# Three fp32 layers on one core: weight conversions beside attention through GpSimd's queue, low words rounded on GpSimd, and a table of leads that orders the ready work

## The chip, the core and the metric

The kernel runs on one core of a Trainium2 chip. Five engines take part, each with an instruction queue of its own: TensorE (PE in the profile; its weight loads are PEld), VectorE (DVE), ScalarE (ACT), GpSimd (POOL) and SyncE (SP), which here issues transfers only. The metric is the device time of one launch in microseconds, the lower the better.

## The reference

```python
scores = scale * np.matmul(q, k.transpose(0, 1, 3, 2)) - np.log(S)   # 4 x 12 heads, S = 448, head_dim 64
attn = 1.0 / (1.0 + np.exp(-scores))
attn_out = np.matmul(attn, v).astype(np.float32)
x = np.ascontiguousarray(attn_out.transpose(0, 2, 1, 3)).reshape(B * S, H * D)   # 1792 tokens x 768
h = x @ w_in                     # 768 x 2048
x = (h * np.cos(h)) @ w_out      # 2048 x 768
g = x @ w_gate                   # 768 x 1536
silu = g * (1.0 / (1.0 + np.exp(-g)))
val = x @ w_val
out = silu * val @ w_out2        # 1536 x 768
```

Sigmoid attention, then a layer with h cos(h), then a gated layer. q, k and v are float32; the five weights come as float64.

## The kernel before

**Precision.** A float32 operand is held as a pair of fp32r tiles, `hi` (a rounded copy) and `lo` (what the copy left out), and a product is three matmuls, hi hi, hi lo and lo hi. Making such a pair takes a copy (mostly on ScalarE) and a subtraction on VectorE.

**Weights.** They lie in memory as 64-bit words. A loop in `conversions` (L419) makes float32 of one tile of 128 x 768 after the other: load the raw words (768 KB, `raw` or `lr`), round the low word to float32 (L430, ScalarE), take the absolute value of the high word (`absolute`, L412, ScalarE or VectorE), clamp it (L435), shift it (L438), put sign and bits together (L441), add the low word as an integer (a custom instruction, `vec` at L230), and store the tile (384 KB) to scratch memory, where `loads` fetches it again whenever a unit wants it. Two such loops run through the MLP; beside attention `lend_pool` (L388) runs four more with tiles `lr0` to `lr3` and `lt0` to `lt3`, which convert 13 tiles. All their transfers are issued by SyncE (`move`, L235), in whose queue the loads of q and k (`rqk`) and v (`vs`) stand too.

**Attention.** 24 pairs of heads, one after the other. VectorE splits the next pair's q and k into `qk` (L723, L724; two buffers), TensorE makes four blocks of scores (L734), ScalarE the sigmoid `a` (L738), and TensorE weighs v with the pair before (L748, sums in `banks`). The pair's output is copied into `R` (rows `r`).

**MLP.** TensorE works through 28 units of two tiles of d_ff; units 0 to 7 are the first layer's first half of the tokens, 8 to 15 its second half, from 16 on comes the second layer. Half and layer together are a stage. A unit is seven products (numbers 1 5 2 6 7 3 4, nine matmuls each of 128 x 448) of sums of operand blocks, which stand for eight plain ones, and between them the down products of the unit before (twelve matmuls each), which need all four `g`. For each unit VectorE and ScalarE make the weight operands (`wa`, `wb`, `s` and one tile in `x1`), and of each result `g`: u, f, the rounding (L816), a sine, a product, the pair `g`. At a change of stage they also make the seven operands `X` of the next stage's tokens from `R` (`inputs`, L640 on): four subtractions into `R`, seven copies `hi` (L658 ScalarE, L660 VectorE) and seven subtractions `lo`, each over 3 x 448 columns. A slot of `X` comes free when its last product of the stage before is done; the last stage's unit still has its down products ahead.

**Order.** Everything beside attention is placed by a list scheduler at build time (`Order`, L74 on). Steps are generators that yield an engine (or several) with an estimated time; of the ready steps the one that can start first is taken, and among equals the one of lowest rank. A rank is mostly a due time in TensorE's plan less a lead that is written out in the code.

```python
key = (start, task.rank)
if best is None or key < best[0]:
    best = key, task, engine, time
```

The program order of each engine is thereby fixed; on the chip an engine that waits holds up all that stands behind it in its own queue. In attention the hand-written steps stand first and the scheduler fills the time between them (`beside`).

## Time and profile before

| what | value |
|---|---|
| median of 3 runs | 1082.96 us (1081.62 to 1082.97) |
| profiled execution | 1087.36 us, span of its core 1085.3 us |
| granted TensorE clock, mean | 0.992 of 2.4 GHz |
| busy: TensorE, VectorE, ScalarE, GpSimd | 98%, 78%, 61%, 11% |
| transfers of SyncE's queue | 155.51 MB, 45.3% of the 16 DMA engines' time |

Times in the rows are from the span's start. Attention takes the first 154 us, the first layer goes to 586 us, the second to the end. The profiled execution is some 4 us longer than the median. Busy shares are averages; where an engine holds up another is read from waits and timeline.

### The profile page before, as it was taken

What the parts mean: (1) busy time and instruction counts of PE and PEld (TensorE: products, weight loads), DVE (VectorE), ACT (ScalarE), POOL (GpSimd) and SP (SyncE); (2) the same over time, 40 slices, a digit from 0 to 9 for tenths busy, and PEclk for the clock granted to TensorE, in tenths of its full rate; (3) what the DMA queues carried; (4) which work ended last, traced back from release to release, by engine and by line L of the source; (5) the groups of instructions that cost most, each with busy time, mean ns of one, the idle gap of its engine ahead of it and who ended that gap; (6) DMA issues with size and microseconds to landing.
All of it is one profiled execution on the core that took longest, in us unless ns stands there. A gap on an engine that the chain in (4) does not pass through costs nothing.

```text
span 1085.3 us, 14759 instructions
## 1 busy us (share of the span) xinstructions
PE 1065.9 (98%) x5507; PEld 933.1 (86%) x5507; DVE 848.9 (78%) x1138; ACT 664.8 (61%) x1005; POOL 124.7 (11%) x97
## 2 busy tenths in 40 slices
PE   9999999999999899999997999999999999999998
PEld 5554569999989799999997999999999999999997
DVE  4969759989999999989899888897559644555643
ACT  6887768877777777777776665554345344433330
POOL 0000002001111101100023100111111210110100
PEclk9999999999999899999998999999999999999999
DMA  9999424545654145454513565655122322112002
GB/s 267 301 264 248 143 88 146 200 150 175 220 202 146 59 161 205 160 188 146 189 59 122 170 221 202 203 189 175 45 73 76 117 85 73 56 48 73 30 1 102
DMA packets 64455, 156.68 MB, mean 144 GB/s; under 512 B 10112, under 2 KB 36736, under 8 KB 64384
## 3 DMA queue, kind: packets, MB, share of 16 engines
q1 hardware_dynamic: 64240, 155.51, 45.3%
q8 instruction: 43, 0.70, 0.3%
q10 hardware_dynamic: 144, 0.23, 0.1%
q14 instruction: 28, 0.23, 0.1%
HBM read 123.47 MB, written 32.24 MB: 143 GB/s over the span
## 4 chain that ended last, share of the span: by engine, by line
PE 88%; DVE 9%; issue 1%; ACT 1%; DMA 0%; DVEq 0%; ACTq 0%
PE banks L1000 42%; PE banks L902 33%; PE banks L748 7%; PE banks L734 6%; DVE x L230 2%; DVE r L230 2%; DVE u L230 1%; DVE g L230 1%; DVE wa L230 1%; DVE wb L230 0%; DMA rqk<-in_qk 0%; DVE u L816 0%; DVE s L230 0%; DVE x L660 0%; ACT x L658 0%
## 5 line engine op out<-in xcount | busy, mean ns | idle before, releaser
L902 PE MATMUL banks<-g,wb 128*128 128x448 f32 x1044 | 224.2, 362 | 1.1 <-ACT g L227 0.6
L1000 PE MATMUL banks<-x,wb 128*128 128x448 f32 x1044 | 224.9, 363 | 0.3 <-ACT banks L227 0.3
L902 PEld LDWEIGHTS banks<-g,wb 128*128 128x128 f32 x1044 | 195.5, 187 | 15.5 <-ACT g L227 1.4
L1000 PEld LDWEIGHTS banks<-x,wb 128*128 128x128 f32 x1044 | 196.8, 189 | 14.0 <-ACT banks L227 0.7
L902 PE MATMUL banks<-g,wa 128*128 128x448 f32 x720 | 160.6, 370 | 9.8 <-ACT g L227 8.5
L1000 PE MATMUL banks<-x,wa 128*128 128x448 f32 x738 | 159.7, 362 | 0.1
L902 PEld LDWEIGHTS banks<-g,wa 128*128 128x128 f32 x720 | 137.9, 192 | 21.3 <-ACT g L227 9.3
L1000 PEld LDWEIGHTS banks<-x,wa 128*128 128x128 f32 x738 | 138.2, 187 | 10.3 <-issue 0.7
L227 ACT ACTIVATE u<-u 128x448 f32<-128x448 f32 x179 | 99.4, 570 | 39.4 <-DVE u L230 26.6
L230 DVE TENSOR_TENSOR u<-u,banks 128x448 f32<-128x448 f32 x119 | 73.4, 617 | 57.1 <-PE banks L1000 54.1
L230 DVE TENSOR_TENSOR r<-banks,r 128x896 f32<-128x896 f32 (+1 forms) x69 | 74.2, 1075 | 50.5 <-PE banks L902 50.0
L738 ACT ACTIVATE a<-banks 128x896 f32<-128x896 f32 x96 | 82.9, 920 | 20.2 <-PE banks L734 12.4
L230 DVE TENSOR_TENSOR wb<-t,wb 128x768 fp32r<-128x768 f32 x73 | 69.5, 956 | 14.9 <-ACT wb L227 14.4
L227 ACT ACTIVATE g<-u 128x448 fp32r<-128x448 f32 x97 | 55.1, 572 | 39.0 <-DVE u L230 23.9
L1000 PE MATMUL banks<-x,s 128*128 128x448 f32 x360 | 78.5, 362 | 0.0
L734 PEld LDWEIGHTS banks<-qk 64*128 64x128 f32 x576 | 51.5, 188 | 29.6 <-ACT a L738 8.2
L227 ACT ACTIVATE wb<-t 128x768 fp32r<-128x768 f32 x73 | 60.9, 837 | 24.6 <-PE banks L1000 17.8
L512 POOL TENSOR_TENSOR sum<-t 128x384 f32<-128x384 f32 x20 | 35.2, 1758 | 339.9 <-DMA t<-swi 78.1
L734 PE MATMUL banks<-qk 64*128 64x448 f32 x576 | 69.9, 386 | 3.5 <-ACT a L738 2.2
L227 ACT ACTIVATE r<-banks 128x896 f32<-128x896 f32 x52 | 47.8, 920 | 41.1 <-PE banks L902 41.0
L1000 PEld LDWEIGHTS banks<-x,s 128*128 128x128 f32 x360 | 67.5, 188 | 4.5
L227 ACT ACTIVATE banks<-banks 128x448 f32<-128x448 f32 x80 | 42.3, 529 | 46.3 <-PE banks L1000 45.1
(103 smaller groups left out, 1476.3 us busy)
## 6 DMA issues: line engine op xcount, KB each, us to landing
raw<-in_w_out SPq DMA_DIRECT2D x23, 768.0 KB, 5.2
t<-swi SPq DMA_DIRECT2D x32, 384.0 KB, 3.2
t<-swo SPq DMA_DIRECT2D x64, 192.0 KB, 2.5
rqk<-in_qk SPq DMA_DIRECT2D x47, 224.0 KB, 7.5
raw<-in_w_gate SPq DMA_DIRECT2D x12, 768.0 KB, 4.6
raw<-in_w_val SPq DMA_DIRECT2D x12, 768.0 KB, 4.9
t<-swg SPq DMA_DIRECT2D x18, 384.0 KB, 3.0
t<-swd SPq DMA_DIRECT2D x34, 192.0 KB, 3.0
```

Source lines behind the costliest of these rows:

```text
L227: return {"ACT": time}, lambda _: nc.scalar.activation(**kw)
L230: return {"DVE": time}, lambda _: nc.vector.tensor_tensor(out=out, in0=in0, in1=in1, op=op)
L512: on.tensor_tensor(out=out, in0=a, in1=b, op=op)
L734: nc.tensor.matmul(sc[:, j], lhsT=both[half, m, 1, starts[c]:starts[c] + P], rhs=both[half, p, 0], start=n == 0, stop=n == 2,)
L738: nc.scalar.activation(out=a, in_=sc, func=AF.Sigmoid, bias=-math.log(S), scale=1.0 / math.sqrt(D))
L748: nc.tensor.matmul(o[half], lhsT=value, rhs=a[:, j], start=c == 0, stop=c == NCH)
L902: nc.tensor.matmul(banks[:, first + e - d, :N], lhsT=w[:, m, e % KH, :], rhs=g[:, 1 - p], start=(i, m, p) == (0, 0, 0) and is_fresh and no ...
L1000: nc.tensor.matmul(bank, lhsT=w[:, m, k, :], rhs=x[p][:, k], start=(k, m, p) == (0, 0, 0) and i in (1, 5), stop=(k, m) == (KH - 1, 1), ski ...
```

## The change

In the three parts of the title, and with new estimates for some steps:

- **Queue.** The loops beside attention issue their raw loads and their stores on GpSimd (`move_beside`), and the plan gives a raw load 9.5 us to land. `begun` lets the four loops begin 4.5 us apart, each behind a one-element copy by GpSimd that reads a tile of q and k. 14 tiles are converted there (13 before), 54 in the MLP (55).
- **Rounding.** The low word is multiplied by 2^-29 and turned into float32 by a `tensor_scalar` of GpSimd in place of ScalarE's activation: 68 instructions.
- **Leads.** The leads come from a table, `LEAD`, whose entries take the place of the numbers in the code; the estimate of a cast of `x` on VectorE goes from 0.9 to 1.55 us, and a product's from 0.203 to 0.2005 a matmul.

TensorE's own order of products is the same. Counted by engine: VectorE casts five `x` (nine before), ScalarE copies 23 (19); VectorE takes 19 absolute values fewer and ScalarE as many more; GpSimd has 68 roundings, 28 transfers and 4 copies more; SyncE has 26 transfers fewer. The other leads are replaced in the same way as the ones shown.

```diff
+LEAD = {
+    "u": 4.53,
+    "f": 4.5,
+    "stt": 3.8,
+    "sin": -0.47,
+    "mult": 2.8,
+    "ghi": -0.12,
+    "glo": 1.06,
+    "whi": 12.36,
+    "wlo": 4.37,
+    "c5": -2.88,
+    "c7": 6.95,
+    "c6": 2.87,
+    "c3": 4.46,
+    "xd": 5.72,
+    "xhi": -8.03,
+    "xlo": -0.1,
+    "sv": 15.9,
+    "acc": -1.59,
+    "bank": 1.82,
+    "first": 1.35,
+    "second": 3.8,
+    "fifth": -3.28,
+    "s22": 6.97,
+    "s12": 6.23,
+    "silu": 3.11,
+    "conv": 21.66,
+}
...
+    def move_beside(out, in_):
+        return {"POOL": 0.9}, lambda _: nc.gpsimd.dma_start(out=out, in_=in_)
+
     LANDING = 5.0
+    LANDING_BESIDE = 9.5
...
-    PRODUCT = 0.203
+    PRODUCT = 0.2005
...
-                uses.setdefault((id(w), 2 * c + i), due[key] - 25.0)
+                uses.setdefault((id(w), 2 * c + i), due[key] - LEAD["conv"])
...
-    def lend_pool():
+    def lend_pool(raw_qk):
...
-            order.spawn(conversions(raw, t, backs[-1], stop), end)
+            order.spawn(begun(a, raw_qk, conversions(raw, t, backs[-1], stop)), end)
...
+    def begun(a, raw_qk, steps):
+
+        yield 6.0 + 4.5 * a
+        yield {"POOL": 0.3}, lambda _: nc.gpsimd.tensor_copy(warm[:, a:a + 1], raw_qk[:, (a + 1) % 4, 1, S - 1:S])
+        yield from steps
...
-        return {"ACT": 0.9, "DVE": 0.58}, do
+        return {"ACT": 0.9, "DVE": 0.61}, do
...
-            yield move(raw.rearrange("p n two -> p (n two)"), flat(w[f]).bitcast(I32))
-            yield LANDING
-            yield by(time, act(0.9, out=raw[:, :, 0], in_=raw[:, :, 0].bitcast(U32), func=AF.Copy, scale=2.0 ** -29))
+            convey = move_beside if back else move
+            yield convey(raw.rearrange("p n two -> p (n two)"), flat(w[f]).bitcast(I32))
+            yield LANDING_BESIDE if back else LANDING
+            yield by(time, ({"POOL": 1.1}, lambda _: nc.gpsimd.tensor_scalar(
+                raw[:, :, 0], raw[:, :, 0].bitcast(U32), 2.0 ** -29, None, op0=ALU.mult
+            )))
             if not back:
                 t = yield convs
             ti = t.bitcast(I32)
             yield by(time, absolute(t, raw[:, :, 1]))
-            yield by(time, ({"DVE": 0.56}, lambda _: nc.vector.tensor_scalar(
+            yield by(time, ({"DVE": 0.62}, lambda _: nc.vector.tensor_scalar(
                 t, t, HI_MOST, HI_LEAST, op0=ALU.min, op1=ALU.max
             )))
...
-            yield by(time, ({"DVE": 0.56}, lambda _: nc.vector.tensor_scalar(
+            yield by(time, ({"DVE": 0.62}, lambda _: nc.vector.tensor_scalar(
...
-            yield move(there[0], t)
+            yield convey(there[0], t)
...
-            yield by(due[keys[0]] - 2.4, copy(0.2 + size / 1200, hi, t))
+            yield by(due[keys[0]] - LEAD["whi"], copy(0.2 + size / 1200, hi, t))
...
-            return {"ACT": 1.32, "DVE": 0.9}, do
+            return {"ACT": 1.32, "DVE": 1.55}, do
...
-                yield by(time - 5.0, vec(1.6, t, parts[0], parts[1], SUB))
+                yield by(time - LEAD["xd"], vec(1.6, t, parts[0], parts[1], SUB))
...
-            yield by(time - 3.2, to_hi(hi, t))
-            yield by(time - 1.7, vec(1.6, lo, t, f32(hi), SUB))
+            yield by(time - LEAD["xhi"], to_hi(hi, t))
+            yield by(time - LEAD["xlo"], vec(1.6, lo, t, f32(hi), SUB))
...
-            stops = [lend_pool()]
+            stops = [lend_pool(raw_qk)]
...
-        yield by(time - 1.5, copy(0.6, g[:, 1], f))
-        yield by(time - 0.8, vec(0.65, g[:, 0], f, f32(g[:, 1]), SUB))
+        yield by(time - LEAD["ghi"], copy(0.6, g[:, 1], f))
+        yield by(time - LEAD["glo"], vec(0.65, g[:, 0], f, f32(g[:, 1]), SUB))
```

**SyncE's queue of before, in attention around pairs 12 to 15.** `rqk` and `vs` are loads of q, k and v, `lr` a raw load, `swi` and `swo` scratch tiles that are stored from `lt` or loaded into `t`.

```order
L708 DMA vs13_675<-in_v 128x384
L716 DMA t_66<-in_v 64x3x64 x2
L236 DMA swi4_674<-lt2_119 128x768
L236 DMA lr2_118<-in_w_in 128x1536
L236 DMA t_66<-swi2_378 128x768
L707 DMA rqk_79<-in_qk 64x2x448 x2
L708 DMA vs14_731<-in_v 128x384
L236 DMA swi5_775<-lt3_121 128x768
L707 DMA rqk_79<-in_qk 64x2x448 x2
L708 DMA vs15_787<-in_v 128x384
```

**GpSimd's queue of after, the same part of attention.** L470 is the rounding of a low word, L268 a transfer.

```order
L268 DMA swo1_612<-lt1_117 128x768
L268 DMA lr1_116<-in_w_out 128x1536
L470 TENSOR_SCALAR lr0_114<-lr0_114 128x768
L268 DMA swi4_728<-lt2_119 128x768
L470 TENSOR_SCALAR lr1_116<-lr1_116 128x768
L268 DMA swi5_730<-lt3_121 128x768
L268 DMA lr2_118<-in_w_in 128x1536
L268 DMA lr3_120<-in_w_in 128x1536
L268 DMA swo2_790<-lt0_115 128x768
L268 DMA lr0_114<-in_w_out 128x1536
```

Stores and raw loads stood between the loads of q, k and v on SyncE; now they stand behind one another on GpSimd, with the roundings between them.

**VectorE of before, ahead of the first down product of unit 6 (place C).** `g` of L230 is what that product waits for; L660 is a cast of `x`, `wb` are weight operands.

```order
L660 CAST x0_72<-r1_65 128x3x448
L816 SCALAR_TENSOR_TENSOR u3_1443<-u5_1449,u3_1443 128x448
L230 TENSOR_TENSOR u0_1440<-u0_1440,u1_1441 128x448
L230 TENSOR_TENSOR g1_1437<-u2_1442,g1_1437 128x448
L230 TENSOR_TENSOR wb0_1446<-t_66,wb0_1446 128x768
L230 TENSOR_TENSOR u3_1443<-u3_1443,banks_63 128x448
L230 TENSOR_TENSOR wb2_1448<-t_66,wb2_1448 128x768
L230 TENSOR_TENSOR g0_1436<-u0_1440,g0_1436 128x448
L230 TENSOR_TENSOR g3_1439<-u3_1443,g3_1439 128x448
```

**VectorE of after, the same place; one `x0_72<-r1_65,x0_72` more stands two rows ahead of the first row.**

```order
L259 TENSOR_TENSOR u3_1456<-u3_1456,u4_1457 128x448
L259 TENSOR_TENSOR r1_65<-r1_65 128x1344
L259 TENSOR_TENSOR x0_72<-r1_65,x0_72 128x3x448
L858 SCALAR_TENSOR_TENSOR u2_1455<-u5_1462,u2_1455 128x448
L259 TENSOR_TENSOR wb0_1459<-t_66,wb0_1459 128x768
L259 TENSOR_TENSOR wb2_1461<-t_66,wb2_1461 128x768
L259 TENSOR_TENSOR u2_1455<-u2_1455,banks_63 128x448
L259 TENSOR_TENSOR u1_1454<-u1_1454,u0_1453 128x448
L259 TENSOR_TENSOR g2_1451<-u3_1456,g2_1451 128x448
L259 TENSOR_TENSOR x0_72<-r1_65,x0_72 128x3x448
L259 TENSOR_TENSOR g0_1449<-u2_1455,g0_1449 128x448
L259 TENSOR_TENSOR g3_1452<-u1_1454,g3_1452 128x448
```

Two `lo` subtractions of `x` (three with the one ahead) and one into `r1` stand before `g0` now, where one cast of `x` stood before; the others followed behind `g3`.

**VectorE of before, ahead of the first down product of unit 15 (place E).** The four rows ahead of these (two `lo` subtractions of `x`, one into `r0`, and L816 with a weight operand) stand behind the accumulation `r1` of the product before.

```order
L230 TENSOR_TENSOR wb2_1448<-t_66,wb2_1448 128x768
L816 SCALAR_TENSOR_TENSOR u2_1442<-u5_1449,u2_1442 128x448
L230 TENSOR_TENSOR wa0_68<-t_66,wa0_68 128x768
L230 TENSOR_TENSOR u0_1440<-u0_1440,banks_63 128x448
L230 TENSOR_TENSOR x1_1325<-r0_64,x1_1325 128x3x448
L816 SCALAR_TENSOR_TENSOR u4_1444<-u5_1449,u4_1444 128x448
L230 TENSOR_TENSOR u2_1442<-u2_1442,u3_1443 128x448
L230 TENSOR_TENSOR g1_1437<-u0_1440,g1_1437 128x448
L230 TENSOR_TENSOR u4_1444<-u4_1444,u1_1441 128x448
L230 TENSOR_TENSOR g0_1436<-u2_1442,g0_1436 128x448
L230 ISA t_66<-raw1_1434,t_66 128x1536
L230 TENSOR_TENSOR g3_1439<-u4_1444,g3_1439 128x448
```

**VectorE of after, the same place.** Ahead of these stand one `lo` subtraction of `x`, one into `r0`, one more `lo` subtraction, behind the same accumulation.

```order
L858 SCALAR_TENSOR_TENSOR u2_1455<-u5_1462,u2_1455 128x448
L259 TENSOR_TENSOR x1_1338<-r0_64,x1_1338 128x3x448
L858 SCALAR_TENSOR_TENSOR u3_1456<-u5_1462,u3_1456 128x448
L259 TENSOR_TENSOR wb2_1461<-t_66,wb2_1461 128x768
L259 TENSOR_TENSOR x1_1338<-t3_1463,x1_1338 128x768
L858 SCALAR_TENSOR_TENSOR u4_1457<-u5_1462,u4_1457 128x448
L259 TENSOR_TENSOR u3_1456<-u3_1456,u1_1454 128x448
L259 TENSOR_TENSOR wa0_68<-t_66,wa0_68 128x768
L259 TENSOR_TENSOR u4_1457<-u4_1457,u0_1453 128x448
L259 TENSOR_TENSOR g0_1449<-u3_1456,g0_1449 128x448
L858 SCALAR_TENSOR_TENSOR u1_1454<-u5_1462,u1_1454 128x448
L259 TENSOR_TENSOR g1_1450<-u4_1457,g1_1450 128x448
```

The same four steps of 3 x 448 columns stand ahead of `g` (all of them now before the first `g`, one between the others before); the integer addition (ISA) that stood between two `g` now follows behind all of them.

## Rows read from the trace of the kernel before

**Rows 1.** Page, section 1: busy us, share of the span, instructions by engine.
```profile
PE 1065.9 (98%) x5507; PEld 933.1 (86%) x5507; DVE 848.9 (78%) x1138; ACT 664.8 (61%) x1005; POOL 124.7 (11%) x97
```

**Rows 2.** Waits of TensorE: who waits <- who releases, us in total, times, longest.
```profile
PE banks L902 <- ACT g L227: 9.1, 3, 5.7
PE banks L734 <- ACT a L738: 2.2, 1, 2.2
PE banks L902 <- DVE g L230: 1.8, 4, 0.7
```

**Rows 3.** Stretches: us, busy PE (x) PEld DVE ACT POOL, PEclk, DMA share, GB/s.
```profile
366.50:371.90 5.40, 5.38 (x14) 4.79 (x15) 3.91 (x5) 2.07 (x5) 2.00 (x1) 0.50 0.49 149
...
591.20:597.20 6.00, 5.96 (x15) 4.96 (x16) 4.38 (x7) 2.55 (x5) 5.84 (x3) 0.50 0.86 304
```

**Rows 4.** Timeline, 96 to 113 us: start, us, engine, operation, [idle before <- releaser].
```profile
97.02 2.48 PE L748 MATMUL banks<-a,vs 128*64 128x448 f32 x12
...
101.86 1.32 ACT L658 ACTIVATE x<-r 128x1344 fp32r<-128x1344 f32 x1 [2.84 <-DVE r L230]
...
104.48 0.87 PE L734 MATMUL banks<-qk 64*128 64x448 f32 x6 [2.19 <-ACT a L738]
...
105.28 4.17 PE L748 MATMUL banks<-a,vs 128*64 128x448 f32 x12
```

**Rows 5.** Waits, 20 to 80 us, the one of VectorE for q and k.
```profile
DVE qk L723 <- DMA rqk<-in_qk: 13.3, 4, 5.0
```

**Rows 6.** Timeline, 74 to 76 us, VectorE.
```profile
74.92 0.63 DVE L723 CAST qk<-rqk 128x896 fp32r<-128x896 f32 x1 [3.93 <-DMA rqk<-in_qk]
```

**Rows 7.** Timeline at the four changes of stage, TensorE and VectorE.
```profile
306.56 0.47 PE L902 MATMUL banks<-g,wb 128*128 128x448 f32 x1 [0.56 <-ACT g L227]
...
337.43 0.95 DVE L230 TENSOR_TENSOR wb<-t,wb 128x768 fp32r<-128x768 f32 x1
...
338.30 1.15 DVE L230 TENSOR_TENSOR g<-u,g 128x448 fp32r<-128x448 f32 x2
...
339.37 3.02 DVE L230 TENSOR_TENSOR x<-r,x 128x1344 fp32r<-128x1344 f32 x2
...
339.51 3.08 PE L902 MATMUL banks<-g,wa 128*128 128x448 f32 x14 [0.69 <-DVE g L230]
...
365.19 0.74 PE L902 MATMUL banks<-g,wa 128*128 128x448 f32 x1 [2.80 <-ACT g L227]
...
591.15 2.27 PE L902 MATMUL banks<-g,wa 128*128 128x448 f32 x4 [5.73 <-ACT g L227]
```

**Rows 8.** Chain that ended last, in order of time: start, us, engine, names, count.
```profile
133.84 2.75 PE banks L734 x24
...
145.66 2.75 PE banks L734 x24
...
176.37 4.80 PE banks L902 x24
```

**Rows 9.** Page, section 6, DMA issues: count, KB, median us from issue to landing.
```profile
lr<-in_w_in SPq DMA_DIRECT2D x8, 768.0 KB, 9.7
```

**Rows 10.** Timeline, 344 to 350 us, GpSimd beside VectorE.
```profile
344.41 1.02 POOL L512 TENSOR_TENSOR t<-t,t 128x384 f32<-128x384 f32 x1 [21.73 <-DVE sum L512]
...
347.11 2.13 DVE L230 TENSOR_TENSOR x<-r,x 128x1344 fp32r<-128x1344 f32 x1
...
347.90 2.22 POOL L512 TENSOR_TENSOR t<-t 128x384 f32<-128x384 f32 x1
```

**Rows 11.** By line and shape, the clamp of a conversion: busy us, mean ns.
```profile
L435 DVE TENSOR_SCALAR t<-t 128x768 f32<-128x768 f32 x27 | 17.1, 633 | 0.5 <-ACT t L412 0.2
...
L435 DVE TENSOR_SCALAR lt<-lt 128x768 f32<-128x768 f32 x13 | 7.2, 553 | 0.0
```

**Rows 12.** Stretch 155 to 567 us, columns as above.
```profile
155.00:567.00 412.00, 406.99 (x2014) 379.19 (x2014) 378.57 (x531) 316.62 (x506) 51.75 (x38) 0.99 0.49 163
```

**Rows 13.** Instructions by line, 155 to 567 us, ScalarE: the rounding of low words.
```profile
L227 ACT ACTIVATE raw<-raw 128x768 int32<-128x768 uint32 x37 | 33.5, 905 | 0.8 <-DMA raw<-in_w_gate 0.4 <-DMA raw<-in_w_out 0.3
```

More of the change, by code (lines that the diff above doesn't have):

```diff
@@ L444, in conversions @@
             ), time
-            yield by(time, vec(0.97, ti, ti, raw[:, :, 0], ADD))
+            yield by(time, vec(1.0, ti, ti, raw[:, :, 0], ADD))
             if not back:
@@ L876, in banker @@
                     acc = R[units[n][1]][:, j, d:d + 2]
-                    yield by(due["down", n, j, d] - 1.3, copy(0.92, banks[:, first:first + 2, :N], acc))
+                    yield by(due["down", n, j, d] - LEAD["bank"], copy(0.92, banks[:, first:first + 2, :N], acc))
                 held[j, d] = first
@@ L930, in first_copy @@
             got["b"] = yield b
-            yield by(due[n, u, 2] - 0.6, copy(0.55, got["b"], got["a"]))
+            yield by(due[n, u, 2] - LEAD["first"], copy(0.55, got["b"], got["a"]))
             copied.set()
@@ L968, in after @@
                     z[ij] = ((yield tmps), order.event())
-                order.spawn(silu(z[ij][0], h, read, z[ij][1], min(time, due["g", n, key[2]] - 6.0)), 0)
+                order.spawn(silu(z[ij][0], h, read, z[ij][1], min(time, due["g", n, key[2]] - LEAD["silu"])), 0)
             else:
```

36 lines of the change are left out of this document (18 added, 18 removed).

## The prediction

> **What bounds the kernel now.** I read the busy totals first: TensorE is at work for 98% of the span [rows 1], so nothing can be won but its waits and the stretches at the lower clock behind them. Then the waits of TensorE: ScalarE's `g` ends 9.1 us of them in three places, VectorE's `g` 1.8 us in four, ScalarE's `a` (the sigmoid of attention) 2.2 us [rows 2]. Then the granted clock: 0.50 (1.2 of 2.4 GHz) in the stretches behind the long waits, 1.00 elsewhere [rows 3].
>
> Place A is in attention, at 102 us. ScalarE stood idle 2.84 us for a VectorE subtraction that feeds `x<-r` (L658), with the next sigmoids queued behind it; TensorE waited 2.19 us, and a group of twelve matmuls that takes 2.48 us then took 4.17 us: 2.19 + 1.69 = 3.9 us [rows 4]. Why VectorE was late: between 20 and 80 us it waited 13.3 us for tiles of q and k. These stand in SyncE's queue behind stores of converted weights, which wait for VectorE [rows 5]; the cast at 74.92 us had stood 3.93 us [rows 6].
>
> Places B to E are where the MLP changes its stage (token half or layer): B at 306 us (0.56 us), C ahead of 339.5 us (0.69), D ahead of 365.2 us (2.80), E ahead of 591.2 us (5.73) [rows 7]; what is left of VectorE's 1.8 us [rows 2] follows B (0.3), D (0.6) and the last unit. TensorE needs `g` for a down product; VectorE, busy without a gap, has made the next stage's `x` (1.5 us a piece) first. A matmul takes 0.2 us at full clock (24 in 4.80 us) [rows 8]. Behind D 15 weight loads ran in 5.40 us where 27 fit, 12 x 0.2 = 2.4 us lost; behind E 16 in 6.00 us, 2.8 us lost [rows 3]. Price of the places: A 3.9, B 0.9, C 0.7, D 5.8, E 8.5, together 19.8 us. The sum is made on the profiled execution, 1087.36 us with a span of 1085.3; that is 4.4 us over the median, and I carry the difference over to 1082.96.
>
> **Attention: the other queue.** The weights' 26 transfers leave SyncE's queue, 28 go into GpSimd's (one tile more is converted here). SyncE then issues q, k and v with nothing before them that waits for VectorE, so the 13.3 us are VectorE's again. What is queued behind a waiting store is now only GpSimd's own work: the next raw load and the rounding of a low word. The four raw loads at the start wait for a tile of q and k each; what is converted from them isn't needed for a hundred us, so this costs nothing. ScalarE loses 13 roundings, and its `x<-r` behind the sigmoids comes one pair earlier, behind three VectorE pieces of 1.5 us in a row that is not late. `qk` has two buffers, so a split of q and k may start when the scores two pairs back are done. From the end of one such block of scores (133.84 + 2.75) to the start of the next but one (145.66) are 9.1 us [rows 8], the split takes 1.7, so VectorE may be 7 us late. I take A as gone: -3.9 us. Landing of a raw tile: 9.7 us from SyncE's queue [rows 9]; from GpSimd's no row shows it. The nearest bound below is the same 9.7, above it twice that, which eats the 7 us; I take 9.7.
>
> **The roundings on GpSimd.** 54 more in the MLP. An addition there moves 3 x 384 elements in 1.02 us at best [rows 10], a rounding 2 x 768: 1.36 us by accesses. The Trainium skill ("GPSIMD Engine Reference", Performance pitfalls for Q7 kernels) would give about 1.9 cycles an element, an estimate of 1.2 us, and no other sum. GpSimd has room (11% busy) [rows 1]. The cost is VectorE's: beside GpSimd's additions its `x` took 2.13 us instead of 1.55, and the clamp of a conversion 0.633 us in the MLP against 0.553 in attention [rows 10, 11]. Bounds for one rounding: 0 and 1.36 us of VectorE; I take the nearest row, 0.58 us for 2.2 us of GpSimd, so 0.36 us, 19 us in all. Against it VectorE loses 17 absolute values in the MLP (ScalarE takes them) and 4 casts of `x`: 17 x 0.5 + 4 x 1.47 = 14 us. From 155 to 567 us VectorE idles 412 - 379 = 33 us, and 37 roundings fall there [rows 12, 13], so this hides, except in the boundaries. If that cover is gone, it is rival 2. ScalarE loses more than these absolute values and casts bring it; its idle time costs nothing.
>
> **The order at the boundaries.** From one start to the next VectorE takes 0.54 us for 448 columns, 0.87 for 768, 1.47 for `x` [rows 7]. I count what the order puts between the release and the `g` waited for; the rows of it stand in the section on the change.
> - C (first down product of unit 6). The slot of the first `x` is free after product 1 of unit 7; 27 matmuls of 5, 2 and 6 and four of the down product follow, 6.2 us, less 0.3 for the release: 5.9 us. Before: one cast, two weight pieces, six of 448: 1.47 + 1.74 + 3.24 = 6.5, 0.6 us late; the trace has 0.69. Now: three `x`, one subtraction, two weight pieces, seven of 448: 5.88 + 1.74 + 3.78 = 11.4, 5.6 us late after 0.1 of tail. ScalarE has three copies of 1.3 us and an absolute value ahead of the same `g`, which adds some 0.6; one rounding falls in, 0.4. I take 6.6, and 2.6 for the clock behind it: 9.2 us.
> - D. Before, VectorE's work from C on is 4.3 us late here, of which the trace shows 0.69 + 2.80 + 0.6. Now the three `x` are done already; the same count gives 3.3 us, less than the wait at C has given back. I take 0.
> - B. Before 1.2 us late by this count (0.9 in the trace). Now VectorE comes over 2 us early: 0.
> - E (52 matmuls, 10.4 us, after the product whose accumulation stands first). Before: four of 1.47, four of 0.87, nine of 448 after 1.3 of release and accumulation: 5.88 + 3.48 + 4.86 + 1.4 - 10.4 = 5.2; the trace has 5.73. Now a conversion's addition and one 448 fewer: 5.88 + 2.61 + 4.32 + 1.4 - 10.4 = 3.8, with the same excess 4.3, and 2.7 for the clock: 7.0 us.
> - A PSUM copy behind the first `x` copy: 0.4 us.
>
> Now: 9.2 + 7.0 + 0.4 = 16.6 us, before 19.8: -3.2 us, so 1079.8 us. With A's 3.9 gone, the MLP itself gets 0.7 us worse.
>
> **Rivals.**
> 1. The wait in attention only moves. GpSimd's queue delivers late, VectorE stands in order before a raw tile, and q and k are split late. It decides when landings exceed about 17 us (9.7 + 7). For: GpSimd's own work took up to 2.2 times as long beside VectorE [rows 10], and 28 issues stand in one line. Against: the 13.3 us given back. Price one more A, 3.9 us: 1083.7. The Trainium skill ("DMA: Bandwidth & Descriptors", SWDGE vs HWDGE vs iDMA) speaks against the change here: GpSimd writes the descriptors into SBUF, where VectorE's two-port modes lock it out; no run here shows such a transfer yet.
> 2. Slower: a rounding stops VectorE for its whole time. 37 x 1.36 = 50 us less 8 us of absolute values, against 33 us of idle: 9 us of new waits in layer 1, 2.6 of clock: 1091.4. It decides from 1.1 us a rounding ((33 + 8) / 37). For: the stretched rows [rows 10, 11]. Against: they show a quarter of that. The skill ("SBUF — State Buffer", Who interferes with whom) says that whoever starts first holds the shared ports and the other fully blocks, by which each rounding would cost 1.36; the trace agrees only in part, +0.58 us beside 2.2 us.
> 3. The wait at C doesn't come: TensorE is already delayed there, or the count overstates. 1079.8 - 9.2 = 1070.6. Against: the count met C, D and E of before within 0.6 us.
>
> **How the numbers follow.** Forecast 0.55 (its own range 1076 to 1084, since C may be 4 us off either way), rival 1 0.17, rival 2 0.15, rival 3 0.13. 0.2% (2.2 us, about what a measurement can tell from no change) puts the bounds at 1080.8 and 1085.1. Faster: 0.37 of the forecast, 0.02 of rival 1, all of rival 3: 0.52. Same: 0.17, 0.12 and nothing more: 0.29. Slower: 0.01, 0.03 and rival 2: 0.19. The range of 8 in 10 runs from 1070 to 1087: the forecast, rival 1 and over half of rival 3.
>
> **What would show it.** Right: no wait of TensorE on `a` near 100 us and few waits of VectorE for q and k; one wait on `g` of 5 to 8 us near 334 us, none at 360; one of about 4 us near 584 us; clock 0.50 behind these two alone; `x<-r` all but five times on ScalarE. Wrong: waits on raw tiles in attention (rival 1), rows of VectorE's conversions above 0.8 us on average and idle time gone from 155 to 567 us (rival 2), no wait near 334 us (rival 3).

## The result and the profile after

The changed kernel takes 1090.34 us (median of 4 runs, 1089.24 to 1090.52), the kernel before 1082.97 us: a ratio of 1.0069 with a 95% interval from 1.0051 to 1.0086, so 7.4 us slower. The prediction said 1079.8 us, with 1070 to 1087 as its range.

Where the time went is read from two rows of each timeline: the first matmul of the MLP (the first one from `x`) and the last matmul. First the profiled execution of before, then the changed kernel (start, us, engine, operation):

```profile
154.50 2.07 PE L1000 MATMUL banks<-x,wa 128*128 128x448 f32 x9
...
1080.46 1.36 PE L902 MATMUL banks<-g,wa 128*128 128x448 f32 x6
```

```profile
157.28 2.08 PE L1042 MATMUL banks<-x,wa 128*128 128x448 f32 x9
...
1082.32 1.36 PE L944 MATMUL banks<-g,wa 128*128 128x448 f32 x6
```

From the first of these matmuls to the end of the last one pass 927.3 us before and 926.4 us after: the MLP is as long as it was. Attention is 2.8 us longer, and more than that against an execution of the kernel before that lies near its median, as the first experiment shows.

The page's busy times by engine, of after; [rows 1] is the line of before:

```profile
PE 1063.5 (98%) x5507; PEld 932.9 (86%) x5507; DVE 863.6 (79%) x1113; ACT 632.0 (58%) x960; POOL 317.1 (29%) x199
```

GpSimd's work went from 124.7 to 317.1 us. Most of it, 176.0 us, is the 68 roundings, in two rows of the view by line and shape (count, busy us, mean ns, idle before):

```profile
L470 POOL TENSOR_SCALAR raw<-raw 128x768 int32<-128x768 uint32 x54 | 138.2, 2559 | 230.5 <-DMA raw<-in_w_gate 57.5
...
L470 POOL TENSOR_SCALAR lr<-lr 128x768 int32<-128x768 uint32 x14 | 37.8, 2698 | 11.1 <-DMA lr<-in_w_out 5.5 <-DMA lr<-in_w_in 4.8
```

A rounding takes 2.56 us in the MLP and 2.70 beside attention; the planner counts 1.1 us, and the prediction 1.36. TensorE's waits of after, beside [rows 2]:

```profile
PE banks L944 <- ACT g L256: 9.4, 2, 4.8
PE banks L776 <- ACT a L780: 4.9, 1, 4.9
PE banks L944 <- DVE g L259: 2.4, 3, 2.1
```

The wait on `a` near 100 us [rows 4] is gone, and one more than twice as long stands at 60 us. The timeline there, TensorE first, then ScalarE, then GpSimd:

```profile
65.54 1.49 PE L776 MATMUL banks<-qk 64*128 64x448 f32 x6 [4.87 <-ACT a L780]
```

```profile
63.41 0.84 ACT L256 ACTIVATE wa<-t 128x768 fp32r<-128x768 f32 x1 [5.98 <-POOL t L554]
64.16 0.53 ACT L792 ACTIVATE r<-banks 128x448 f32<-128x448 f32 x1
```

```profile
53.89 1.02 POOL L554 TENSOR_TENSOR t<-t 128x384 f32<-128x384 f32 x1
55.00 2.80 POOL L470 TENSOR_SCALAR lr<-lr 128x768 int32<-128x768 uint32 x1
57.88 1.10 POOL L554 TENSOR_TENSOR t<-sum,t 128x384 f32<-128x384 f32 x1
59.06 3.05 POOL L470 TENSOR_SCALAR lr<-lr 128x768 int32<-128x768 uint32 x1
62.20 1.18 POOL L554 TENSOR_TENSOR t<-t 128x384 f32<-128x384 f32 x1
```

These are the lines to read: the sums of weight blocks for the first operands of the MLP (L554) stand in GpSimd's queue with the roundings between them, so two roundings hold the last sum up by 5.85 us. ScalarE's copy `wa<-t` waits 5.98 us for that sum; the sigmoids stand behind the copy in ScalarE's queue; TensorE waits 4.87 us for a sigmoid. Behind that wait the granted clock is at half (1.2 of 2.4 GHz), as a stretch of it shows (columns as in [rows 3]):

```profile
66.00:68.00 2.00, 2.00 (x10) 0.91 (x10) 1.97 (x4) 1.10 (x2) 1.36 (x1) 0.50 0.99 364
```

Six matmuls of the scores take 1.49 us there in place of 0.87 [rows 4], and the next block of `a` and `vs` 4.49 us in place of the 3.16 of an earlier one, in the chain of waits (start, us, what):

```profile
43.45 3.16 PE banks L790 x16
...
67.03 4.49 PE banks L790 x16
```

That is 1.95 us more, so this place costs 4.87 + 1.95 = 6.8 us.

The MLP's waits of after stand where the prediction had them, `g` at C and E and none at B and D:

```profile
345.83 0.47 PE L944 MATMUL banks<-g,wa 128*128 128x448 f32 x1 [4.82 <-ACT g L256]
348.39 5.20 PE L944 MATMUL banks<-g,wa 128*128 128x448 f32 x14 [2.10 <-DVE g L259]
...
594.23 0.74 PE L944 MATMUL banks<-g,wa 128*128 128x448 f32 x1 [4.62 <-ACT g L256]
595.12 4.15 PE L944 MATMUL banks<-g,wa 128*128 128x448 f32 x11 [0.15 <-DVE g L259]
```

And the clock behind C and E, in stretches (columns as in [rows 3]):

```profile
348.00:350.00 2.00, 1.61 (x4) 1.48 (x5) 2.00 (x3) 1.54 (x3) 1.92 (x2) 0.50 0.00 0
350.00:352.00 2.00, 2.00 (x7) 1.74 (x7) 2.00 (x2) 1.54 (x2) 1.92 (x2) 0.50 0.00 0
...
596.00:598.00 2.00, 2.00 (x7) 1.74 (x6) 2.00 (x5) 1.38 (x3) 1.96 (x1) 0.50 0.02 6
```

### The profile page after: what moved, and what is told of

Its sections match the earlier page's. It is cut to its first block, busy times and chain, and to the rows that moved or that the text cites. A ratio compares the mean times of both kernels' runs of the same rounds, so it can differ in the third digit from the quotient of the medians.

```text
span 1087.5 us, 14896 instructions
## 1 busy us (share of the span) xinstructions
PE 1063.5 (98%) x5507; PEld 932.9 (86%) x5507; DVE 863.6 (79%) x1113; ACT 632.0 (58%) x960; POOL 317.1 (29%) x199
## 4 chain that ended last, share of the span: by engine, by line
PE 93%; DVE 4%; POOL 1%; ACT 1%; issue 1%; DMA 0%; ACTq 0%; POOLq 0%; DVEq 0%
PE banks L1042 44%; PE banks L944 36%; PE banks L790 7%; PE banks L776 6%; DVE x L259 1%; DVE r L259 1%; POOL lr L470 1%; DMA rqk<-in_qk 0%; DVE u L259 0%; DVE g L259 0%; DVE wa L259 0%; POOL t L554 0%; DVE wb L259 0%; ACT x L700 0%; DVE u L858 0%
## 5 line engine op out<-in xcount | busy, mean ns | idle before, releaser
L470 POOL TENSOR_SCALAR raw<-raw 128x768 int32<-128x768 uint32 x54 | 138.2, 2559 | 230.5 <-DMA raw<-in_w_gate 57.5
L944 PE MATMUL banks<-g,wa 128*128 128x448 f32 x720 | 160.2, 369 | 11.7 <-ACT g L256 9.4
L256 ACT ACTIVATE g<-u 128x448 fp32r<-128x448 f32 x97 | 55.3, 573 | 59.7 <-DVE u L259 33.8
L259 DVE TENSOR_TENSOR g<-u,g 128x448 fp32r<-128x448 f32 x97 | 64.4, 668 | 13.2 <-ACT g L256 13.2
L554 POOL TENSOR_TENSOR t<-t 128x384 f32<-128x384 f32 x25 | 30.6, 1226 | 145.3 <-DVE sum L554 70.9
```

Source lines behind the costliest of these rows:

```text
L256: return {"ACT": time}, lambda _: nc.scalar.activation(**kw)
L259: return {"DVE": time}, lambda _: nc.vector.tensor_tensor(out=out, in0=in0, in1=in1, op=op)
L470: yield by(time, ({"POOL": 1.1}, lambda _: nc.gpsimd.tensor_scalar(raw[:, :, 0], raw[:, :, 0].bitcast(U32), 2.0 ** -29, None, op0=ALU.mult)))
L554: on.tensor_tensor(out=out, in0=a, in1=b, op=op)
L944: nc.tensor.matmul(banks[:, first + e - d, :N], lhsT=w[:, m, e % KH, :], rhs=g[:, 1 - p], start=(i, m, p) == (0, 0, 0) and is_fresh and no ...
```

## The experiments

Every time is a median, with its ratio to the kernel before, measured beside it, and the 95% interval. "MLP start" and "MLP length" are read as above from the profiled execution of each.

| run | time, us | ratio to before (95%) | MLP start | MLP length |
|---|---|---|---|---|
| changed kernel | 1090.34 | 1.0069 (1.0051 to 1.0086) | 157.28 | 926.4 |
| e1, kernel before again | 1082.42 | 0.9985 (0.9968 to 1.0003) | 151.72 | 925.8 |
| e2, sums on VectorE | 1086.60 | 1.0024 (1.0009 to 1.0038) | 156.51 | 925.4 |
| e3, 2.7 us planned everywhere | 1106.09 | 1.0206 (1.0172 to 1.0240) | 150.62 | 947.5 |
| e4, attention's roundings on ScalarE, planned anew | 1091.89 | 1.0071 (1.0053 to 1.0090) | 150.59 | 936.8 |
| e5, the same, plan untouched | 1087.21 | 1.0037 (1.0024 to 1.0050) | 157.17 | 926.2 |
| e6, MLP's roundings on ScalarE, plan untouched | 1090.50 | 1.0066 (1.0051 to 1.0081) | 158.29 | 927.0 |
| e7, transfers on SyncE, plan untouched | 1089.38 | 1.0052 (1.0036 to 1.0068) | 157.88 | 926.2 |
| e8, before with roundings on GpSimd | 1091.68 | 1.0079 (1.0063 to 1.0095) | 152.21 | 932.1 |
| e9, 2.7 us planned beside attention | 1084.17 | 1.0007 (0.9994 to 1.0019) | 152.74 | 927.2 |
| e10, before with the queue alone | 1090.17 | 1.0066 (1.0053 to 1.0078) | 158.26 | 928.2 |
| e11, e9 and five other leads | 1082.11 | 0.9989 (0.9978 to 1.0000) | 154.20 | 923.4 |
| e12, e10 with the first loads spaced | 1083.79 | 1.0004 (0.9986 to 1.0021) | 153.38 | 925.8 |
| e13, e4 and twelve other leads | 1084.12 | 1.0001 (0.9986 to 1.0016) | 150.36 | 928.5 |

Two kinds of edit are in it. Where the planner sees the edit (e2, e3, e4, e9, e11, e13), it may set everything behind it in another order. "Plan untouched" (e5 to e8, e10, e12) means that the planner counts as before and only the engine to which an instruction is issued differs, so that all the other orders stay row for row.

**e1: what does a usual execution of the kernel before look like?** No edit.

> The kernel before, unchanged, for more executions of it. Theory: the wait A (2.19 us and 1.69 us of clock at 102 us) belongs to the one execution that was profiled, 4.4 us over its median; then a profile near the median of 1083 us starts the MLP at 150.6 us in place of 154.5 and has no wait of TensorE on `a` over 1 us. Rival: A is in every execution and the 4.4 us lie elsewhere; then the MLP starts at 154.5 us again and the spans near 1081 have A too.

```profile
103.36 0.87 PE L734 MATMUL banks<-qk 64*128 64x448 f32 x6 [1.23 <-ACT a L738]
...
151.72 2.08 PE L1000 MATMUL banks<-x,wa 128*128 128x448 f32 x9
```

This profile is of an execution of 1082.83 us. Place A is there, but at 1.23 us and with no stretch at half clock behind it, and the MLP starts at 151.72 us: between the theory (150.6) and its rival (154.5). So A costs 1.2 us in this execution near the median; the 3.9 us that the prediction took for it belonged to the execution profiled first, which was 4.4 us over the median. Against this one the changed kernel's attention is 157.28 - 151.72 = 5.6 us longer: A's 1.2 gone and 6.8 new, which makes 5.6 as well. The MLP is 0.6 us longer, and the two profiled executions (1089.24 and 1082.83 us) are 6.4 us apart, so these two places leave next to nothing over. The two profiles of the kernel before differ by 1.5 us in the MLP alone; a smaller difference of two MLP lengths tells nothing.

**e9: is it the planned time of a rounding?**

```diff
-            yield by(time, ({"POOL": 1.1}, lambda _: nc.gpsimd.tensor_scalar(
+            yield by(time, ({"POOL": 2.7 if back else 1.1}, lambda _: nc.gpsimd.tensor_scalar(
```

> The changed kernel with one number changed, and only beside attention: there the planner takes 2.7 us for a rounding on GpSimd in place of 1.1. Every engine's order in the MLP stays the same; beside attention ScalarE's copy of `wa` is planned one pair of heads later or more. Theory (the copy stands too early because a rounding is planned at 1.1 us and takes 2.7): no wait of TensorE over 1 us in attention behind the first pair, MLP start 150.5 to 151.2 us in place of 157.3, MLP 925.4 to 926.9 us, time 1082.5 to 1085. Rival (VectorE or the landings of q and k are late by themselves, as where the sums went to VectorE): MLP start 154 to 157 us, time 1086 to 1090.

```profile
55.04 0.52 ACT L256 ACTIVATE s<-sum 128x384 fp32r<-128x384 f32 x1 [3.06 <-POOL sum L554]
...
56.85 0.87 PE L776 MATMUL banks<-qk 64*128 64x448 f32 x6 [1.63 <-ACT a L780]
```

With one number that says how long a rounding really takes, attention is 4.5 us shorter and the time falls by 6.2 us, to that of the kernel before. The MLP's orders are the same in both, and its length differs by 0.8 us. So most of the loss hangs on that number: ScalarE's copy stood where the planner believed the sum to be done. The new plan not only sets the copies of `wa` later, it also gives two of the four sums of this place to VectorE; which of the two gave the time back, this run does not separate. The theory's bound is missed in one point: a wait of 1.63 us stays, for the copy of `s` ahead of the sigmoids; its sum waited 3.83 us for a load of `t`.

**e3: the same number everywhere.**

```diff
-            yield by(time, ({"POOL": 1.1}, lambda _: nc.gpsimd.tensor_scalar(
+            yield by(time, ({"POOL": 2.7}, lambda _: nc.gpsimd.tensor_scalar(
```

> The changed kernel with one number changed: the planner takes 2.7 us for a rounding on GpSimd in place of 1.1. Theory (the plan's estimate lets ScalarE's copy stand too early): the copy of `wa` is planned one pair of heads later, the wait at 65 us falls from 4.87 to under 1 us, the MLP starts near 151 us; the order in the MLP changes too, by up to 4 us either way, time 1080 to 1087. Rival (VectorE late by itself): 1087 to 1091 with a new wait in attention.

```profile
374.44 0.74 PE L944 MATMUL banks<-g,wa 128*128 128x448 f32 x1 [9.86 <-ACT g L256]
```

Attention is free of the wait (start 150.62, as the theory had it), and the MLP, ordered anew, is 21 us longer, far outside the expected 4 us either way: D alone waits 9.86 us for `g`. A truer estimate made a worse order, since the leads were set for the old one.

**e2: no sums on GpSimd beside attention.** The planner may give them to VectorE only, until attention ends.

```diff
-            return {"DVE": 0.6, "POOL": 1.3}, do, time
+            return ({"DVE": 0.6, "POOL": 1.3} if source[0].time is not None and order.now > PAIR * NP * B + 6.0 else {"DVE": 0.6}), do, time
```

> The changed kernel, but until attention ends the sums of weight blocks (L554) are made by VectorE only, so that no ScalarE copy waits for GpSimd's queue. Theory (two roundings of 2.8 and 3.05 us between GpSimd's sums make ScalarE's copy of `wa` 5.98 us late, with the sigmoids behind it): the 4.87 us wait at 65 us and the clock behind it (0.50 from 64 to 70 us) go, the MLP starts at 150.5 to 152 us in place of 157.3, time 1083 to 1085. Rival (VectorE, stretched by GpSimd, is late by itself): a wait on `a` or `qk` of over 2 us comes elsewhere in attention, time 1087 to 1091.

```profile
61.54 0.74 PE L776 MATMUL banks<-qk 64*128 64x448 f32 x2 [3.50 <-DVE qk L765]
```

```profile
47.10 13.55 DMA rqk<-in_qk
60.65 0.03 issue
...
60.77 0.64 DVE qk L765
```

The wait on `a` is gone, and one of 3.50 us on `qk` stands four us earlier. The second fence is the chain of waits (start, us, what): a load of q and k took 13.55 us from issue to landing, where the changed kernel's median is 8.0. So the rival's sign is there, a wait of over 2 us elsewhere, though not its reason: with GpSimd's sums out of the way it is the landing of q and k that ends the next wait, and not a VectorE that is late by itself.

**e4 and e5: the roundings beside attention on ScalarE**, planned there (e4) and only issued there (e5). The new `rounded_by(low, on_act)` issues the same multiplication to ScalarE or to GpSimd. First e4, then e5:

```diff
+            if back:
+                yield by(time, act(0.9, out=raw[:, :, 0], in_=raw[:, :, 0].bitcast(U32), func=AF.Copy, scale=2.0 ** -29))
+            else:
...
```

```diff
-            yield by(time, ({"POOL": 1.1}, lambda _: nc.gpsimd.tensor_scalar(
...
+            yield by(time, ({"POOL": 1.1}, lambda _: rounded_by(raw[:, :, 0], bool(back))))
```

> The changed kernel with the 14 roundings beside attention on ScalarE as before; GpSimd's queue, the leads and the 54 roundings in the MLP stay. Theory: GpSimd's sums come in time, no wait over 1 us on `a`, MLP start near 151 us, time 1081 to 1085. Rival (the transfers in GpSimd's queue, not the roundings, delay what stands behind them): the wait stays over 3 us, time 1087 to 1091.

> The changed kernel with the plan untouched, so every engine's order stays as it is, but the 14 roundings beside attention are issued to ScalarE at their planned places. Theory (roundings of 2.7 us in GpSimd's queue make its sums late, ScalarE's copy of `wa` and the sigmoids behind it late): the wait at 65 us goes, the MLP starts between 150.6 and 152 us in place of 157.3, time 1083.5 to 1085.5. Rival (q and k late by the transfers of two queues, as a landing of 13.55 us showed where the sums were moved to VectorE): a wait on `qk` or `a` of 2 to 4 us remains, time 1086.5 to 1089.

Of e5, the last of the four sums on GpSimd, ScalarE's copy of `wa` that needs it, and two of TensorE's waits:

```profile
59.65 1.74 POOL L558 TENSOR_TENSOR t<-t 128x384 f32<-128x384 f32 x1
```

```profile
61.42 0.84 ACT L256 ACTIVATE wa<-t 128x768 fp32r<-128x768 f32 x1
```

```profile
57.68 0.87 PE L780 MATMUL banks<-qk 64*128 64x448 f32 x6 [1.76 <-ACT a L784]
78.06 0.87 PE L780 MATMUL banks<-qk 64*128 64x448 f32 x6 [0.82 <-ACT a L784]
```

In e4 attention has no wait left behind its first pair and the MLP starts at 150.59 us, the lowest but one of all runs: the transfers in GpSimd's queue are not what held the sums up. The time is worse because the MLP was ordered anew (936.8 us). e5 is the cleaner test, since only the roundings change their engine: without them between the sums, these follow one another on GpSimd, the copy `wa<-t` waits for nothing that the profile shows (5.98 us in the changed kernel), and TensorE's wait of 4.87 us is gone. So the roundings in GpSimd's queue are its cause. The 1.76 us belong to the copy of `s` one pair earlier, the place that also waits in e9. The rest of the theory, start and time, is missed: 14 roundings of 0.92 us now stand among sigmoids in an order that had no room for them, and the profiled execution, the slowest of its six, has five waits on `a` (3.6 us together), one of 1.8 us on the first `qk`, and a start of 157.17 us. The median is 3.1 us below the changed kernel's.

**e6 and e8: what does a rounding cost VectorE?** Only the issuing engine differs: e6 gives the MLP's 54 roundings to ScalarE, e8 gives all 68 of the kernel before to GpSimd.

```diff
-            yield by(time, ({"POOL": 1.1}, lambda _: nc.gpsimd.tensor_scalar(
...
+            yield by(time, ({"POOL": 1.1}, lambda _: rounded_by(raw[:, :, 0], not back)))
```

```diff
-            yield by(time, act(0.9, out=raw[:, :, 0], in_=raw[:, :, 0].bitcast(U32), func=AF.Copy, scale=2.0 ** -29))
+            yield by(time, ({"ACT": 0.9}, lambda _: nc.gpsimd.tensor_scalar(
+                raw[:, :, 0], raw[:, :, 0].bitcast(U32), 2.0 ** -29, None, op0=ALU.mult
+            )))
```

> The changed kernel with the plan untouched, but the 54 roundings of the MLP are issued to ScalarE at their planned places; those beside attention stay on GpSimd. Theory (a rounding takes some 0.4 us of VectorE's time, hidden but at the changes of stage): VectorE's busy time falls by 54 x 0.4 = 22 us, the waits at C (6.92) and E (4.77) by at most 1 us each, time 1088 to 1090. Rival 2 (a rounding stops VectorE for its whole 2.56 us): busy time falls by over 100 us and the time by over 5 us, to 1085 or less.

> The kernel before with its plan untouched, but all 68 roundings issued to GpSimd at their planned places. Theory: in the MLP little changes (0.4 us of VectorE a rounding, at most 1.5 us at the four changes of stage); beside attention each conversion is 1.7 us later, and SyncE's stores hold the loads of q and k longer: the MLP starts 1 to 5 us later than 151.7, time 1084 to 1090. Rival 2 (whole time of VectorE): the MLP alone takes over 5 us more than 925.8. Rival (GpSimd has room, nothing waits): 1082 to 1084.

The busy times of e6, then of e8:

```profile
PE 1064.4 (98%) x5507; PEld 931.9 (86%) x5507; DVE 840.3 (77%) x1113; ACT 671.0 (62%) x1014; POOL 180.6 (17%) x145
```

```profile
PE 1064.0 (98%) x5507; PEld 931.2 (86%) x5507; DVE 884.5 (81%) x1138; ACT 612.3 (56%) x937; POOL 318.4 (29%) x165
```

VectorE executes the same instructions in e6 as in the changed kernel and is busy 840.3 in place of 863.6 us. Not all of the 23.3 us lie in the MLP, where the 54 roundings are. The stretch from the MLP's first matmul to the end of its last one, the changed kernel's and then e6's (columns as in [rows 3]):

```profile
157.28:1083.70 926.42, 913.96 (x4538) 853.16 (x4536) 737.16 (x976) 526.00 (x828) 255.77 (x144) 0.99 0.40 131
```

```profile
158.29:1085.30 927.01, 913.03 (x4538) 852.55 (x4536) 716.41 (x977) 565.18 (x882) 117.81 (x90) 0.99 0.39 131
```

737.16 - 716.41 = 20.75 us for 54 roundings are 0.38 us for one of 2.56 us. Beside attention it is more. Up to the MLP's start, the changed kernel and then e5:

```profile
0.00:157.28 157.28, 149.54 (x971) 79.78 (x972) 125.85 (x136) 106.04 (x132) 61.28 (x56) 0.97 0.77 221
```

```profile
0.00:157.17 157.17, 149.94 (x972) 79.21 (x972) 114.80 (x136) 116.39 (x146) 24.97 (x42) 0.98 0.77 221
```

125.85 - 114.80 = 11.05 us are 0.79 us for each of the 14; against e6, which has the same 14 and is busy 123.27 us there, it is 0.60. In e8 it is 884.5 - 847.8 (e1) = 36.7 us for 68 of both kinds, 0.54 us each. The prediction had 0.36 for the MLP; rival 2, in which VectorE stands still for the whole rounding, would need over 130 us in e6.

What that costs depends on the order. In the changed kernel it costs nothing that is seen: with the roundings back on ScalarE the MLP is 0.6 us longer, which tells nothing (e1), and the waits at C, which were to fall, are 7.24 and 1.14 us in place of 4.82 and 2.10, since the copy of `g` on ScalarE comes later. In the order of before the MLP of e8 is 6.2 us longer than that of e1, as its rows at B and C show beside the 0.56 and 0.69 us of [rows 7]:

```profile
306.49 0.47 PE L904 MATMUL banks<-g,wb 128*128 128x448 f32 x1 [2.61 <-ACT g L227]
...
341.20 0.47 PE L904 MATMUL banks<-g,wa 128*128 128x448 f32 x1 [2.40 <-ACT g L227]
```

There `g` was already late behind a VectorE without a gap, so each stretched instruction counts; this reason is read from the order and not tested by itself. The theory allowed for 1.5 us, and over 5 us was the sign set for rival 2. But 0.54 us of VectorE for a rounding is not its whole time, so the sign came without rival 2's mechanism.

**e7, e10 and e12: what is the queue worth?** e7 issues the changed kernel's 28 transfers on SyncE, e10 those of the kernel before on GpSimd, and e12 puts each of e10's first four raw loads behind a copy that reads a tile of q and k, as `begun` does.

The edits of e7, of e10 (its raw loads are led over in the same way as the stores shown) and of e12:

```diff
-        return {"POOL": 0.9}, lambda _: nc.gpsimd.dma_start(out=out, in_=in_)
+        return {"POOL": 0.9}, lambda _: nc.sync.dma_start(out=out, in_=in_)
```

```diff
+    def move_beside(out, in_):
+        return {"SP": 0.8}, lambda _: nc.gpsimd.dma_start(out=out, in_=in_)
...
-            yield move(there[0], t)
+            yield (move_beside if back else move)(there[0], t)
```

```diff
+    def move_first(out, in_, behind=None):
+        def do(_):
+            if behind:
+                a, raw_qk = behind
+                nc.gpsimd.tensor_copy(warm[:, a:a + 1], raw_qk[:, (a + 1) % 4, 1, S - 1:S])
+            nc.gpsimd.dma_start(out=out, in_=in_)
...
```

> The changed kernel with the plan untouched, but the 28 transfers beside attention are issued by SyncE at their planned places among the loads of q, k and v. Theory (the wait at 65 us comes from the roundings, not from the issues in GpSimd's queue; the other queue frees the loads of q and k): the wait at 65 us stays over 3 us, and VectorE waits for q and k again, over 12 us in attention, time 1090 to 1095. Rival (the issues hold GpSimd up): the wait at 65 us falls under 2 us, time 1085 to 1088.

> The kernel before with its plan untouched, but the 26 transfers beside attention are issued by GpSimd at their planned places; roundings on ScalarE, leads as before. Theory (the queue by itself does what it is for): VectorE's waits for q and k fall from 16.6 us to under 8, the wait A at 102 us goes, MLP start 150.5 to 151 us in place of 151.7, time 0.5 to 2 us under the kernel before. Rival 1 of the prediction (landings from GpSimd's queue too late): VectorE waits for raw tiles, A stays or grows, time 0 to 4 us over the kernel before.

> The kernel before with its plan untouched: the 26 transfers beside attention are issued by GpSimd at their planned places, and each of the first four raw loads behind a one-element copy that reads a tile of q and k, as in the changed kernel. Theory (the 5.69 us at 17 us came from four raw loads at once, and the queue by itself removes the wait at 102 us): no wait over 1 us in attention behind the first pair, MLP start 150.4 to 151 us, MLP 925.8, time 0.5 to 2 us under the kernel before. Rival (transfers of two queues delay q and k anyway): a wait on `qk` or `a` of 1.5 to 6 us, MLP start 152 to 157 us, time the same as before or up to 5 us over it.

e7: the wait stays (5.58 us, up to 66.58 us), so the issues in GpSimd's queue don't make it. VectorE waits 9.0 us for q and k in attention, 7.1 in the changed kernel; over 12 were expected, and the time, within 1 us of the changed kernel's, is just below the expected 1090. So in this plan the queue gives VectorE 1.9 us, by one profile each. In the plan of before it gives nothing clear: e1 waits 16.6 us for q and k, e10 15.1 and e12 16.7, where under 8 were expected of e10. In e10 and e12 the wait at 102 us is indeed gone, and a new one has come, at 17 us in the one and at 61 us in the other:

```profile
16.75 0.74 PE L737 MATMUL banks<-qk 64*128 64x448 f32 x2 [5.69 <-DVE qk L726]
```

```profile
60.86 0.47 PE L746 MATMUL banks<-qk 64*128 64x448 f32 x2 [1.53 <-DVE qk L735]
```

with the loads of q and k on which these waits end, from the chains of e10 and of e12:

```profile
2.91 12.97 DMA rqk<-in_qk
```

```profile
43.47 16.50 DMA rqk<-in_qk
```

With four raw loads issued at once q and k land after 12.97 us, and the spacing takes that first wait away: e12 is 6.4 us faster than e10. But even so the queue gains nothing, 1083.79 against 1083.37 us, as e12's rival had it; e10, at 6.7 us over the kernel before, lies outside both of its ranges. What speaks for a reason is a row of the kernel before that the prediction didn't look at (stretch 0 to 100 us; the last but one column is the share of the DMA engines):

```profile
0.00:100.00 100.00, 97.56 (x635) 52.16 (x635) 74.36 (x92) 76.31 (x95) 3.92 (x8) 1.00 1.03 278
```

The 16 DMA engines are full (share 1.03). In one queue q and k stand behind what was issued before them; in two, the engines would serve the weights and q and k side by side, so that q and k are issued sooner and land later. The Trainium skill ("DMA: Bandwidth & Descriptors", Queues, rings and completion order) says that each engine goes round the queues for which it has work, packet by packet; the landings agree with it, but do not show it. In the four profiles with one queue (both of before, e7, e8) the longest landing of a load of q and k is 11.7 to 14.0 us, in the eleven with two 14.0 to 18.2 us; the medians overlap. For the changed kernel and for e7, which differ in the queue alone (all 48 loads; the page's row, with its median of 8.0, has SyncE's 47):

```profile
DMA to landing us min/median/max: 3.4/7.3/14.1
```

```profile
DMA to landing us min/median/max: 3.4/7.6/11.7
```

**e11 and e13: another order of the MLP.** e11 is e9 with five leads changed; e13 is e4 with the twelve entries of the table changed that its expectation names.

```diff
-    "c7": 6.95,
+    "c7": 12.32,
...
-    "c3": 4.46,
+    "c3": 1.73,
...
-    "sv": 15.9,
+    "sv": 17.97,
...
-    "bank": 1.82,
+    "bank": 1.7,
...
-    "conv": 21.66,
+    "conv": 19.39,
```

> The changed kernel with 2.7 us for a rounding beside attention and five leads changed (c7 6.95 to 12.32, c3 4.46 to 1.73, sv 15.9 to 17.97, bank 1.82 to 1.7, conv 21.66 to 19.39), which order the MLP anew: by the count of VectorE's and ScalarE's work between release and `g`, place C (6.9 us of waits and 2.6 of clock) is met in time, D is 1 to 2 us late, E 5 to 7. Theory (the MLP's waits follow from what stands ahead of `g`, so they can be counted from the order): MLP 918 to 923 us in place of 926.4, start 150.6, time 1075 to 1081. Rival (what the order gives at C is taken again elsewhere): MLP 926 or more, time 1083 to 1087.

> The changed kernel with the 14 roundings beside attention on ScalarE and eleven leads changed (stt, sin, mult, whi, wlo, c7, c6, c3, sv, bank, second, conv), so that by the count of work between release and `g` C is 1 us late, D in time, E 5 us late. Theory (both parts can be counted and add up): MLP start 150.5 to 151 us, MLP 918 to 923 us, time 1071 to 1077. Rival (GpSimd's roundings cost VectorE more at these places than the count has): MLP 924 to 932, time 1077 to 1086.

The rows of e11 at D and E, then those of e13 behind C:

```profile
362.28 0.47 PE L944 MATMUL banks<-g,wa 128*128 128x448 f32 x1 [1.75 <-ACT g L256]
...
587.25 0.74 PE L944 MATMUL banks<-g,wa 128*128 128x448 f32 x1 [6.17 <-ACT g L256]
```

```profile
353.14 2.67 PE L947 MATMUL banks<-g,wa 128*128 128x448 f32 x12 [1.89 <-ACT banks L256]
357.63 1.48 PE L947 MATMUL banks<-g,wa 128*128 128x448 f32 x6 [1.82 <-ACT banks L256]
```

In e11 C waits no longer, D 1.75 and E 6.17 us, as counted from the order, and the MLP is 3 us shorter than the changed kernel's (923.4, where 918 to 923 was expected). Its attention has waits of 1.5 and 1.6 us on `a` again (start 154.20), so the time is 1082.11 us and not under 1081: 8.2 us faster than the changed kernel and 1.4 us below the kernel before, at the edge of what these runs can tell. In e13 attention has the lowest start of all, but the MLP is 928.5 us, and the count missed: ScalarE's copies into `banks` ahead of down products come 1.9 and 1.8 us late, on which it had not counted. Time and MLP are those of the rival, but its reason, VectorE beside the roundings, is not what these rows name.

## Why the prediction was wrong

**The step that failed** is the one on attention's queues: "What is queued behind a waiting store is now only GpSimd's own work: the next raw load and the rounding of a low word", and from it "I take A as gone: -3.9 us". Four things are wrong with it.

- GpSimd's own work is more than that. The sums of weight blocks (L554) for the MLP's first operands stand in the same queue, ScalarE waits for them in order, and TensorE for ScalarE. The chain costs 6.8 us. e5, which takes the roundings out of that queue and leaves the orders, takes the wait of 4.87 us away; e9, which plans the roundings beside attention at their true length, gets 6.2 us of the 7.4 us back. The profiles of e6 and e7, whose plan for attention is the changed kernel's, have the same chain: the copy waits 5.23 and 7.04 us (in e7 the two roundings also wait 1.64 and 2.62 us for their raw tiles).
- The size of a rounding. The term was 1.36 us of GpSimd, worked out from additions "by accesses"; it measured 2.56 and 2.70 us in the mean, 2.21 at the shortest. With 1.36 in place of 2.80 and 3.05 us the sum would have been 3.1 us earlier and the wait of TensorE, by an estimate from these rows, about 1.7 us. What a rounding takes from VectorE beside attention stands in no term; it is 0.6 to 0.8 us, some 8 to 11 us in all.
- A was priced from one execution that was 4.4 us over the median. The prediction said so of the sum and carried the whole difference over, but A's 3.9 us were part of that difference: in the execution near the median it is 1.2 us (e1).
- The other queue does not by itself give VectorE its waits back. "SyncE then issues q, k and v with nothing before them that waits for VectorE, so the 13.3 us are VectorE's again": with the queue alone (e10, e12) VectorE waits for them in attention as long as before, 15.1 and 16.7 against 16.6 us (e1).

Rival 1 named the right kind of end ("the wait in attention only moves", 1083.7) by the wrong road: landings from GpSimd's queue are 9.4 and 10.1 us (medians of the changed kernel), as the forecast took them, and no raw tile holds VectorE up for long (2.2 us in all). Its road is real on the kernel before, for q and k in place of raw tiles (e10, e12). Its price, one more A, was 2.9 us too small.

**The roundings** cost VectorE 0.38 us in the MLP where 0.36 was predicted. That is luck: the length was taken 1.9 times too short (1.36 for 2.56 us) and VectorE's share of it 1.8 times too large (0.58 of 2.2 us for 0.38 of 2.56). And 33.8 us of idle time remain to it between 158 and 570 us, where 33 us stood before: the change in VectorE's sum was small, as worked out. The clamp's mean in the MLP is 0.66 and 0.70 us, under the 0.8 that would have spoken for rival 2. Its 1091.4 us lies near the measured time only by chance: its place, the MLP of the first layer, is not longer. But e8 shows that the same roundings in the old order do cost 6.2 us in the MLP, so that nothing of it shows holds for this order and not for any.

**The MLP** came out as worked out. C: 4.82 + 2.10 us of waits and, behind them, 14 matmuls in 5.20 us where 26 fit, 12 x 0.2 = 2.4; 9.3 us, predicted 9.2. E: 4.62 + 0.15 and 9.75 x 0.2 = 2.0 for 11 in 4.15 us; 6.8 us, predicted 7.0. A copy into `banks` 0.44, predicted 0.4. B and D: no wait, as predicted. Together 16.5 us, predicted 16.6; the MLP's length changes by -0.9 us against the first profile of before and by +0.6 against e1, where +0.7 was predicted; both lie within the 1.5 us by which the two profiles of the kernel before differ. Rival 3 is out.

**What stays open:** why q and k sometimes land after 13 us or more and mostly after 8, with one queue too, and with it how much of attention's spread from run to run (A between 1.2 and 3.9 us) it makes; no run here separates the packets of the two queues. That a rounding would be shorter with the low words packed was not tried.

## What to carry to other kernels

A step that moves to an engine with room must be checked against what already stands in that engine's queue, not against its busy share: GpSimd, at 11% of the span before and 29% after, held TensorE up through a sum, a copy and a sigmoid, because two instructions of three microseconds each stood between its sums. In a kernel whose order a planner fixes, an estimate that is wrong by 1.6 us moves a wait onto the path, and correcting it everywhere may cost 21 us elsewhere (e3), since leads are set for the estimates they were found with. Before a gain from a second queue is counted, look whether the transfer engines are full, and price a wait from more than one execution.
